# Giving out the PSUM banks anew in the last third of a retention and soft mixture-of-experts kernel

## The chip, the cores and the metric

The kernel runs on one core of one Trainium2 chip. The metric is the device time of one execution in microseconds (us); less is better. The profile is one execution taken by the hardware profiler; its times are counted from the start of its span.

## The reference, cut to what matters

All data are fp32. The attention part is a retention (causal scores with a decay, no softmax) over B = 8, H = 8, S = 576, D = 64. Its output is taken as x with N = 4608 rows and 512 features, and a soft mixture of experts with 8 experts of 4 slots each follows:

```python
logits = x @ phi                              # 4608 x 32
d = exp(logits - logits.max(0)); d /= d.sum(0) + 1e-09
slot_input = (d.T @ x).reshape(8, 4, 512)     # the fold over all rows
for e in range(8):
    h = maximum(slot_input[e] @ w1[e], 0.0)   # 4 x 1024
    slot_out[e] = h @ w2[e]                   # 4 x 512
c = exp(logits - logits.max(1)); c /= c.sum(1) + 1e-09
return c @ slot_out.reshape(32, 512)          # 4608 x 512
```

## The kernel before

The 4608 rows are 36 tiles of 128 rows; four tiles are a group, so there are nine groups (NG = 9). A loop over the 36 tiles (lines 290 to 330) computes the retention of a tile, and, one group late, its logits, its share of the sum over rows (`slot_sums`, with a running maximum) and its combine weights, which stay in `lt`. Everything is scheduled by hand: each engine runs its instructions in the order in which the program issues them, and the framework adds the waits that the data and the PSUM buffers ask for.

Behind the loop come four stages, and the change is in them.

- **The fold** (lines 343 to 397) does the last group. `pm` is a transpose of the maxima, `e_transpose` and `slot_sums` make the group's sums in `acc` (line 262), `dl` and `lrun` (lines 373, 374) rescale them, and two products, `pd` (line 377) and `psi` (line 391), followed by two VectorE operations (line 394), give the experts' inputs `sims`.
- **W1** (lines 420 to 439): 32 weight units of 512 KB stay in SBUF. Eight steps of four units make the two halves of the hidden layer, `ph[:, 0]` and `ph[:, 1]`, two banks of one PSUM tile. A half is copied to `h1` by ScalarE (line 436) and VectorE (line 437). A unit that has been used is released: the buffer takes one of the 19 weight units that are still to come (line 81, on SyncE's queue), or goes to the list `free`.
- **W2** (`expert_2`, line 452): for each half k of the output columns 16 units of 512 KB are summed up in one PSUM tile; `slot_out(k)` copies it (line 458), multiplies it by a selection matrix (line 462) and copies the result to `so` (line 463).
- **Results** (`final(k, g)`, lines 467 to 479): for each k and each of the nine groups four products (eight PE instructions, line 474) fill one half, 256 columns of each bank, of two PSUM tiles of two banks, `po[0]` and `po[1]`. ScalarE copies `po[0]` (line 476), VectorE `po[1]` (line 477) into a free SBUF buffer, and SyncE issues its 512 KB store (line 478). There are 18 of these. Those of k = 0 are strewn between the W2 units of k = 1, one result after every two units; those of k = 1 come at the end, one after another.

PSUM has eight banks. The pool `ps_x` has two buffers of two banks (tiles named sx), `ps_st` one bank (pst), `ps_t` three banks (pt), given out in turn. The pools stay as they are to the end, so the results use the four banks of `ps_x` all the time.

Of the kernel before, what the change touches and what calls it, by code (L numbers as in the profile page):

```python
# [8 lines left out]
F32 = mybir.dt.float32  # L9
# [6 lines left out]
P = 128  # L16
# [3 lines left out]
NS = NE * NSE  # L20
NCH = 5
NT = 36
NG = NT // 4
# [3 lines left out]
W = 256  # L27
# [10 lines left out]
def retention_softmoe(ctx, tc, qkv, wts, phi, mtab, vtab, gtab, ctab, msel, out):  # L38
    nc = tc.nc
    PS = bass.MemoryType.PSUM  # L40
# [3 lines left out]

    cpool = ctx.enter_context(tc.tile_pool(name="cpool", bufs=1))
    small = ctx.enter_context(tc.tile_pool(name="small", bufs=2))
    ps_x = ctx.enter_context(tc.tile_pool(name="ps_x", bufs=2, space=PS))
    ps_st = ctx.enter_context(tc.tile_pool(name="ps_st", bufs=1, space=PS))
    ps_t = ctx.enter_context(tc.tile_pool(name="ps_t", bufs=3, space=PS))

    def const(name, *shape):
        return cpool.tile([P, *shape], F32, name=name)
# [16 lines left out]
    lt = const("lt", NG, P)  # L69
# [42 lines left out]
    for a in range(NP):  # L112
        r = slice(0, D) if a % 2 else slice(D, P)
# [91 lines left out]
    def x_transpose(t, pt=None, eng=None):  # L205
        if pt is None:
            pt = ps_t.tile([P, 512], F32, name="pt")
        for a in range(NP):
            nc.tensor.transpose(pt[:, a * P:(a + 1) * P], xT[t][:, a * P:(a + 1) * P], ident)  # L209
        if eng is nc.vector:  # L210
            nc.vector.tensor_copy(out=xT[t], in_=pt)
        else:
            nc.scalar.copy(out=xT[t], in_=pt)  # L213

    def sm(name, n=1):
        return small.tile([P, n], F32, name=name)
# [36 lines left out]
    def slot_sums(g, pp=None):  # L253
        if pp is None:
            pp = ps_t.tile([P, 512], F32, name="pt")
        for i in range(4):
            nc.tensor.matmul(pp[i * NS:(i + 1) * NS, :], lhsT=ens[:, i * NS:(i + 1) * NS], rhs=xT[4 * g + i],  # L257
                             start=True, stop=True, skip_group_check=True)
        if g == 0:
            nc.vector.tensor_copy(out=acc, in_=pp)  # L260
        else:
            nc.vector.scalar_tensor_tensor(out=acc, in0=acc, scalar=galpha[g], in1=pp, op0=ALU.mult, op1=ALU.add)
# [3 lines left out]
    def comb_1(g):  # L266
        pn = ps_t.tile([P, 512], F32, name="pt")[:, 0:P]
        nc.tensor.transpose(pn, lt[:, g, :], ident)  # L268
        ln = pn.rearrange("p (i s) -> p i s", i=4)
        cmx = sm("cmx", 4)  # L270
        nc.vector.tensor_reduce(out=cmx, in_=ln, axis=AX.X, op=ALU.max)
        cc = cn.rearrange("p (i s) -> p i s", i=4)
        nc.vector.tensor_tensor(out=cc, in0=ln, in1=cmx.unsqueeze(2).broadcast_to([P, 4, NS]), op=ALU.subtract)
        nc.scalar.activation(out=cn, in_=cn, func=AF.Exp, scale=1.0)

    def comb_2(g):
        cc = cn.rearrange("p (i s) -> p i s", i=4)
        sv = sm("csm", 4)
        nc.vector.tensor_reduce(out=sv, in_=cc, axis=AX.X, op=ALU.add)
        nc.vector.tensor_scalar(out=sv, in0=sv, scalar1=1e-9, scalar2=None, op0=ALU.add)  # L280
        ri = sm("cri", 4)
        nc.vector.reciprocal(out=ri, in_=sv)
        nc.vector.tensor_tensor(out=cc, in0=cc, in1=ri.unsqueeze(2).broadcast_to([P, 4, NS]), op=ALU.mult)

    def comb_3(g):
        pc = ps_t.tile([P, 512], F32, name="pt")[:, 0:P]
        nc.tensor.transpose(pc, cn, ident)
        nc.scalar.copy(out=lt[:, g, :], in_=pc)
# [3 lines left out]
    for i in range(NT):  # L292
        g, r = divmod(i - 4, 4)
# [20 lines left out]
        if i == NT - 1:  # L314
            pl = ps_st.tile([P, 512], F32, name="pst")[:, 0:P]
# [21 lines left out]
    sims = rg[2]  # L337
# [3 lines left out]
    sims = sims.rearrange("p (k c e s) -> p k c e s", k=2, c=2, e=NE)  # L341

    g = NG - 1
# [9 lines left out]
    nc.scalar.activation(out=ets, in_=pl, func=AF.Exp, bias=nn, scale=1.0, accum_out=rs)  # L353
    x_transpose(4 * g + 2, eng=nc.vector)
    x_transpose(4 * g + 3, eng=nc.vector)
    pm = ps_t.tile([P, 512], F32, name="pt")[:, 0:P]
    nc.tensor.transpose(pm, nn.broadcast_to([P, P]), ident)
    e_transpose(g)
    alpha = sm("alpha")
# [5 lines left out]
    nc.vector.tensor_tensor(out=nq, in0=nf, in1=far, op=ALU.add)  # L365
    nfp = sm("nfp")
    nc.vector.tensor_reduce(out=nfp, in_=nq, axis=AX.X, op=ALU.min)
    slot_sums(g)
    fa = sm("fa")
    nc.scalar.activation(out=fa, in_=nn, func=AF.Exp, bias=nfp, scale=-1.0)  # L370
    nc.scalar.copy(out=lt[:, g, :], in_=pl)
    dl = sm("dl", NS)
    nc.vector.tensor_scalar(out=dl, in0=delta[:, 0:NS], scalar1=fa, scalar2=None, op0=ALU.mult)
    nc.vector.scalar_tensor_tensor(out=lrun, in0=lrun, scalar=alpha, in1=rs, op0=ALU.mult, op1=ALU.add)
    comb_3(g - 1)
    pd = ps_t.tile([P, 512], F32, name="pt")
    nc.tensor.matmul(pd[:, 0:NS], lhsT=lrun.broadcast_to([P, P]), rhs=dl, start=True, stop=True)
# [4 lines left out]
    def diag(a, n, m):  # L382
        v = a[:, :, 0:1].unsqueeze(3).broadcast_to([P, n, m, NSE])
        ap = [list(x) for x in v.ap]
        ap[2][0] = NS + NSE
        ap[3][0] = 1
        return bass.AP(tensor=v.tensor, offset=v.offset, ap=ap)

    psi = ps_t.tile([P, 512], F32, name="pt")
    for c in range(4):  # L390
        nc.tensor.matmul(psi[:, c * P:c * P + NS], lhsT=acc[:, c * P:(c + 1) * P], rhs=dl, start=True, stop=True,
                         skip_group_check=True)
    for k in range(2):
        nc.vector.tensor_tensor(
            out=diag(sims[:, k].rearrange("p c e s -> p c (e s)"), 2, NE),
# [5 lines left out]
    h1 = rg[1].rearrange("p (n f) -> p n f", n=2)  # L401
    free = []

    def release(t):
        if not load_w(t):
            free.append(t)
# [10 lines left out]
            else:  # L417
                nc.scalar.activation(out=dst, in_=src, func=AF.Relu)

    ph = ps_x.tile([P, 2, 512], F32, name="sx")  # L420
    for n in range(8):
        nh, eh, kp = n // 4, n // 2 % 2, n % 2
        if n == 1:
            comb_1(g)
            comb_2(g)
        if n == 3:
            comb_3(g)
        for c in range(2):
            for i in range(4):
                w = unit_tile[4 * n + i].rearrange("p (c f) -> p c f", c=2)  # L430
                nc.tensor.matmul(ph[i * NS:(i + 1) * NS, nh, :], lhsT=sims[:, kp, c, 4 * eh + i, :], rhs=w[:, c, :],  # L431
                                 start=(n % 4 == 0 and c == 0), stop=(n % 4 == 3 and c == 1), skip_group_check=True)
        for i in range(4):
            release(unit_tile[4 * n + i])
        if n % 4 == 3:
            nc.scalar.copy(out=h1[:, nh, 0:256], in_=ph[:, nh, 0:256])
            nc.vector.tensor_copy(out=h1[:, nh, 256:512], in_=ph[:, nh, 256:512])
        if n == 5:
            hidden_out(0, None)

    so = kts
# [3 lines left out]
    def expert_2(k, n):  # L445
        fh, e = divmod(n, NE)
        if n == 0:
            pp2[k] = ps_t.tile([P, 512], F32, name="pt")[:, 0:W]
        u = unit_tile[32 + k * 16 + n]
        w = u.rearrange("p (c f) -> p c f", c=4)  # L450
        for i in range(4):
            nc.tensor.matmul(pp2[k][i * NS:(i + 1) * NS, :], lhsT=hm[fh][:, i, e, :], rhs=w[:, i, :],  # L452
                             start=(n == 0), stop=(n == 2 * NE - 1), skip_group_check=True)
        release(u)

    def slot_out(k):
        lo, hi = k * W, (k + 1) * W
        nc.scalar.copy(out=p2s[:, lo:hi], in_=pp2[k])
        if k == 0:
            expert_2(1, 0)  # L460
        pso = ps_t.tile([P, 512], F32, name="pt")[:, 0:W]
        nc.tensor.matmul(pso, lhsT=delta, rhs=p2s[:, lo:hi], start=True, stop=True)
        nc.scalar.copy(out=so[:, lo:hi], in_=pso)

    po = [ps_x.tile([P, 2, 512], F32, name="sx") for _ in range(2)]

    def final(k, g):
        lo, hi = k * W, (k + 1) * W
        o = free.pop(0)
        ov = o.rearrange("p (i f) -> p i f", i=4)  # L470
        b = slice(g % 2 * W, (g % 2 + 1) * W)
        for i in range(4):
            r = slice(i * NS, (i + 1) * NS)
            nc.tensor.matmul(po[i // 2][:, i % 2, b], lhsT=lt[r, g, :], rhs=so[r, lo:hi], start=True, stop=True,  # L474
                             tile_position=(i * NS, 0), skip_group_check=True)
        nc.scalar.copy(out=ov[:, 0:2], in_=po[0][:, :, b])  # L476
        nc.vector.tensor_copy(out=ov[:, 2:4], in_=po[1][:, :, b])  # L477
        nc.sync.dma_start(out=out[k, g], in_=o)
        free.append(o)

    for n in range(8):
        expert_2(0, n)
        if n == 1:
            hidden_out(1, None)
    for n in range(8, 16):
        expert_2(0, n)
    slot_out(0)
    n = 1
    for g in range(NG):
        if g:  # L490
            final(0, g - 1)
        for _ in range(2):
            if n < 16:
                expert_2(1, n)
                n += 1
    final(0, NG - 1)
    while n < 16:
        expert_2(1, n)
        n += 1
    slot_out(1)  # L500
    for g in range(NG):
        final(1, g)
    man.close()


# [70 lines left out]
```

## Time and profile before

| | |
|---|---|
| median of 3 runs | 239.07 us (237.6 to 240.0) |
| profiled execution, device time | 237.61 us |
| its span, first to last instruction | 235.8 us |
| busy share of the span: PE, VectorE, ScalarE | 92%, 49%, 33% |
| mean granted TensorE clock | 0.948 of full speed |

PE is TensorE's matmuls and PEld its weight loads, DVE is VectorE, ACT ScalarE, POOL GpSimd, SP SyncE. In the rows a group of instructions is named by line, engine, operation and tiles (written <- read); "x8" is their count, and in brackets stands how long the engine was idle before it and what ended that wait. A granted clock of 1.00 is 2.4 GHz, 0.50 is 1.2 GHz.

### The profile page before, as it was taken

The page shows a single profiled execution, that of the slowest core. Times are in us where ns is not written, and L with a number is a line of the kernel's source. Part 1 is how long each engine was busy: PE and PEld are TensorE (multiplying, and loading weights), DVE is VectorE, ACT ScalarE, POOL GpSimd, SP SyncE. Part 2 cuts the span into 40 slices and gives each one's busy share as a digit, 9 for nine tenths or more (in the row PEclk, how much of TensorE's full clock was granted, in tenths as well). Part 3 has the DMA queues.
Part 4 walks back from the last instruction along what each step waited for, and adds up shares of the span by engine and source line. Part 5 has one row for each costly group of instructions (what it writes and reads, how often), then busy time and mean ns, then how long its engine had stood idle before and what let it go on. Part 6 is the DMA issues. An engine that isn't in the chain of part 4 may idle for free.

```text
span 235.8 us, 8980 instructions
## 1 busy us (share of the span) xinstructions
PE 216.4 (92%) x3994; PEld 160.4 (68%) x3994; DVE 116.3 (49%) x234; ACT 77.5 (33%) x191; POOL 61.2 (26%) x65
## 2 busy tenths in 40 slices
PE   7698879999999999899999999999698999986892
PEld 7587768897897887787897896887432354442450
DVE  1255527667556567738557649557640011343331
ACT  2122334254344353353353452351301012333220
POOL 1544444334244252531353423403100000000000
PEclk9889999999999999999999999999999999996555
DMA  6999978799888889878889887986529999786664
GB/s 199 400 421 406 409 299 273 276 343 360 310 275 315 289 325 344 301 259 289 285 326 353 324 314 277 314 326 220 178 76 410 414 410 375 297 332 272 256 256 202
DMA packets 18181, 72.59 MB, mean 308 GB/s; under 512 B 2272, under 2 KB 2528, under 8 KB 18144
## 3 DMA queue, kind: packets, MB, share of 16 engines
q1 hardware_dynamic: 17568, 71.47, 81.1%
q8 instruction: 31, 0.51, 0.8%
q10 hardware_dynamic: 576, 0.56, 0.7%
q14 instruction: 6, 0.05, 0.1%
HBM read 62.58 MB, written 9.44 MB: 305 GB/s over the span
## 4 chain that ended last, share of the span: by engine, by line
PE 83%; DMA 7%; ACT 3%; DVE 3%; issue 2%; SPq 1%; DVEq 0%
PE sx L189 15%; PE sx L162 11%; PE sx L474 8%; PE pt L153 8%; DMA qb<-in_qkv 7%; PE pt L209 7%; PE sx L431 6%; PE pt L452 6%; PE pst L201 6%; PE sx L181 5%; PE pt L257 3%; PE pt L223 3%; ACT ws L476 2%; PE pst L223 1%; PE pt L268 1%
## 5 line engine op out<-in xcount | busy, mean ns | idle before, releaser
L141 POOL TENSOR_TENSOR qb<-qb,vt 128x512 f32<-128x512 f32 x36 | 37.7, 1048 | 85.8 <-DMA qb<-in_qkv 56.9
L166 DVE TENSOR_TENSOR sts<-sx,mt 128x512 f32<-128x512 f32 x72 | 46.3, 684 | 17.1 <-PE sx L162 17.0
L189 PE MATMUL sx<-sts,qb 128*64 128x128 f32 x576 | 40.5, 283 | 1.0 <-DVE sts L166 0.9
L192 DVE TENSOR_TENSOR rg<-sx,xt 128x512 f32<-128x512 f32 x36 | 24.9, 692 | 29.9 <-PE sx L189 28.3
L154 ACT COPY kts<-pt 128x512 f32<-128x512 f32 x36 | 21.1, 587 | 55.7 <-PE pt L153 53.9
L189 PEld LDWEIGHTS sx<-sts,qb 128*64 128x64 f32 x576 | 31.4, 139 | 11.7 <-issue 6.6
L162 PE MATMUL sx<-qb,kts 64*64 64x64 f32 (+1 forms) x1152 | 32.8, 252 | 0.7 <-ACT kts L154 0.7
L162 PEld LDWEIGHTS sx<-qb,kts 64*64 64x64 f32 x1152 | 27.5, 135 | 3.8 <-ACT kts L154 1.1
L477 DVE COPY ws<-sx 128x512 f32<-128x512 f32 x18 | 12.5, 692 | 28.6 <-PE sx L474 27.7
L153 PE MATMUL pt<-ident,qb 128*128 128x128 f32 x144 | 24.0, 290 | 2.5 <-DMA qb<-in_qkv 2.5
L474 PE MATMUL sx<-kts,lt 32*128 32x256 f32 x144 | 21.9, 561 | 3.2 <-ACT ws L476 2.6
L203 ACT COPY sbs<-pst 128x256 f32<-128x256 f32 x32 | 11.9, 372 | 36.6 <-PE pst L201 36.6
L201 PE MATMUL pst<-qb 128*64 128x64 f32 x512 | 20.7, 225 | 0.0
L181 PE MATMUL sx<-qb,sbs 64*64 64x128 f32 (+1 forms) x512 | 18.2, 257 | 2.7 <-issue 2.7
L153 PEld LDWEIGHTS pt<-ident,qb 128*128 128x128 f32 x144 | 15.5, 143 | 7.5 <-issue 4.8
L474 PEld LDWEIGHTS sx<-kts,lt 32*128 32x128 f32 x144 | 10.9, 237 | 14.0 <-ACT ws L476 11.7
L201 PEld LDWEIGHTS pst<-qb 128*64 128x64 f32 x512 | 19.8, 141 | 0.0
L213 ACT COPY rg<-pt 128x512 f32<-128x512 f32 x33 | 17.9, 597 | 4.4 <-PE pt L209 4.4
L143 POOL TENSOR_TENSOR xt<-gt,cf 128x512 f32<-128x512 f32 x16 | 16.7, 1041 | 8.8 <-DVE rg L192 7.0
L209 PE MATMUL pt<-ident,rg 128*128 128x128 f32 x144 | 18.8, 273 | 0.0
L476 ACT COPY ws<-sx 128x512 f32<-128x512 f32 x18 | 10.5, 586 | 20.9 <-PE sx L474 19.8
L209 PEld LDWEIGHTS pt<-ident,rg 128*128 128x128 f32 x144 | 16.2, 140 | 0.4 <-issue 0.4
(87 smaller groups left out, 177.9 us busy)
## 6 DMA issues: line engine op xcount, KB each, us to landing
ws<-in_wts SPq DMA_DIRECT2D x57, 512.0 KB, 7.0
qb<-in_qkv SPq DMA_DIRECT2D x35, 768.0 KB, 5.8
out<-ws SPq DMA_DIRECT2D x18, 512.0 KB, 2.6
qb<-in_wts SPq DMA_DIRECT2D x6, 512.0 KB, 4.3
qb<-in_qkv SPq DMA_DIRECT2D x3, 256.0 KB, 3.7
sts<-in_wts SPq DMA_DIRECT2D x1, 512.0 KB, 5.0
mt<-in_mtab ACTq DMA_DIRECT2D x1, 256.0 KB, 3.9
gt<-in_gtab ACTq DMA_DIRECT2D x1, 256.0 KB, 7.1
```

What stands on the lines that cost most here:

```text
L141: nc.gpsimd.tensor_tensor(out=v, in0=v, in1=vt[:, c, :].unsqueeze(2).broadcast_to([P, H, D]), op=ALU.mult)
L153: nc.tensor.transpose(pt[:, a * P:(a + 1) * P], part(t, 0)[:, a * P:(a + 1) * P], ident)
L154: nc.scalar.copy(out=kts, in_=pt)
L162: nc.tensor.matmul(sp[R[z], j, a, lo:P], lhsT=kT[R[j], a, z * D:(z + 1) * D], rhs=qT(t)[R[j], a, lo:P], start=True, stop=True, skip_group_ ...
L166: nc.vector.tensor_tensor(out=sT[:, j].rearrange("p (s o) i -> p s o i", s=2), in0=sp[:, j].rearrange("p (s o) i -> p s o i", s=2), in1=m, ...
L181: nc.tensor.matmul(x[R[a % 2], j, a // 2, cols], lhsT=sb[R[j], y, a, :], rhs=qT(t)[R[j], a, cols], start=(a < 2 and y == (0 if z == 2 else ...
L189: nc.tensor.matmul(x[R[a % 2], j, a // 2, :], lhsT=vn(t)[:, 2 * a + j, :], rhs=sT[:, j, a, :], start=(c == 0 and a < 2), stop=True, skip_g ...
L192: nc.vector.tensor_tensor(out=xT[t].rearrange("p (j s i) -> p j s i", j=2, s=2), in0=x, in1=xtab(t).rearrange("p (j s) i -> p j s i", j=2) ...
L201: nc.tensor.matmul(pst[R[j], z, a, :], lhsT=kn(t)[:, 2 * a + j, :], rhs=vn(t)[:, 2 * a + j, :], start=(c == 0 and z == 0 and a == 0), stop ...
L209: nc.tensor.transpose(pt[:, a * P:(a + 1) * P], xT[t][:, a * P:(a + 1) * P], ident)
L213: nc.scalar.copy(out=xT[t], in_=pt)
L474: nc.tensor.matmul(po[i // 2][:, i % 2, b], lhsT=lt[r, g, :], rhs=so[r, lo:hi], start=True, stop=True, tile_position=(i * NS, 0), skip_gro ...
```

## The change

Four edits, all behind the loop over the tiles:

1. In the fold, `pm` takes a buffer of `ps_x` in place of one of `ps_t`. `slot_sums` and the copy of the last logits to `lt` are issued behind `fa`, `dl` and `lrun` and not ahead of them.
2. Ahead of W1 all PSUM pools are closed, and two are opened: `ps_a` with two tiles of two banks, and one of four single banks. The two halves of W1's output are a tile each.
3. `slot_out(0)` has two W2 units ahead of its product and two behind it. The results 0 to 5 of k = 0 are computed in pairs, both halves of the columns of `ps_a`'s tiles at once, with four W2 units behind each pair; 6 and 7 lie inside `slot_out(1)`.
4. Then the four single banks are closed, and a second set, `ps_b`, of two tiles of two banks is opened in their place. Result 8 of k = 0 and the nine of k = 1 use `ps_b` and `ps_a` in turn.

```diff
-    pm = ps_t.tile([P, 512], F32, name="pt")[:, 0:P]
+    pm = ps_x.tile([P, 2, 512], F32, name="sx")[:, 0, 0:P]
...
-    slot_sums(g)
     fa = sm("fa")
     nc.scalar.activation(out=fa, in_=nn, func=AF.Exp, bias=nfp, scale=-1.0)
-    nc.scalar.copy(out=lt[:, g, :], in_=pl)
     dl = sm("dl", NS)
     nc.vector.tensor_scalar(out=dl, in0=delta[:, 0:NS], scalar1=fa, scalar2=None, op0=ALU.mult)
     nc.vector.scalar_tensor_tensor(out=lrun, in0=lrun, scalar=alpha, in1=rs, op0=ALU.mult, op1=ALU.add)
+    slot_sums(g)
+    nc.scalar.copy(out=lt[:, g, :], in_=pl)
     comb_3(g - 1)
...
-    ph = ps_x.tile([P, 2, 512], F32, name="sx")
+    stage.close()
+    ps_a, rest = psum("ps_a", 2), ExitStack()
+    ps_t = rest.enter_context(tc.tile_pool(name="ps_g", bufs=4, space=PS))
+    ph = [ps_a.tile([P, 2, 512], F32, name="po")[:, 0] for _ in range(2)]
...
-                nc.tensor.matmul(ph[i * NS:(i + 1) * NS, nh, :], lhsT=sims[:, kp, c, 4 * eh + i, :], rhs=w[:, c, :],
+                nc.tensor.matmul(ph[nh][i * NS:(i + 1) * NS, :], lhsT=sims[:, kp, c, 4 * eh + i, :], rhs=w[:, c, :],
...
-    def slot_out(k):
+    def slot_out(k, between):
         lo, hi = k * W, (k + 1) * W
         nc.scalar.copy(out=p2s[:, lo:hi], in_=pp2[k])
-        if k == 0:
-            expert_2(1, 0)
+        between[0]()
         pso = ps_t.tile([P, 512], F32, name="pt")[:, 0:W]
         nc.tensor.matmul(pso, lhsT=delta, rhs=p2s[:, lo:hi], start=True, stop=True)
         nc.scalar.copy(out=so[:, lo:hi], in_=pso)
-
-    po = [ps_x.tile([P, 2, 512], F32, name="sx") for _ in range(2)]
...
+        between[1]()
+
+    def final(pool, k, *gs):
         lo, hi = k * W, (k + 1) * W
...
+        po = [pool.tile([P, 2, 512], F32, name="po") for _ in range(2)]
+        os = [free.pop(0) for _ in gs]
+        for n, g in enumerate(gs):
+            for i in range(4):
+                r = slice(i * NS, (i + 1) * NS)
+                nc.tensor.matmul(po[i // 2][:, i % 2, n * W:(n + 1) * W], lhsT=lt[r, g, :], rhs=so[r, lo:hi],
+                                 start=True, stop=True, tile_position=(i * NS, 0), skip_group_check=True)
+        for n, g in enumerate(gs):
+            ov = os[n].rearrange("p (i f) -> p i f", i=4)
+            nc.scalar.copy(out=ov[:, 0:2], in_=po[0][:, :, n * W:(n + 1) * W])
+            nc.vector.tensor_copy(out=ov[:, 2:4], in_=po[1][:, :, n * W:(n + 1) * W])
+            nc.sync.dma_start(out=out[k, g], in_=os[n])
+            free.append(os[n])
...
+    slot_out(0, [lambda: experts_2(1, 0, 2), lambda: experts_2(1, 2, 4)])
+    for g in (0, 2, 4):
+        final(ps_a, 0, g, g + 1)
+        experts_2(1, 2 * g + 4, 2 * g + 8)
+    slot_out(1, [lambda: final(ps_a, 0, 6), lambda: final(ps_a, 0, 7)])
+    rest.close()
+    ps_b = psum("ps_b", 2)
+    final(ps_b, 0, 8)
     for g in range(NG):
...
+        final(ps_b if g % 2 else ps_a, 1, g)
```

## Rows read from the trace of the kernel before

**Rows 1.** The page's forty slices: TensorE clock in tenths, DMA GB/s.

```profile
PEclk9889999999999999999999999999999999996555
GB/s 199 400 421 406 409 299 273 276 343 360 310 275 315 289 325 344 301 259 289 285 326 353 324 314 277 314 326 220 178 76 410 414 410 375 297 332 272 256 256 202
```

**Rows 2.** The timeline in the fold: start, duration, engine, line, operation.

```profile
167.62 0.30 PE L250 MATMUL pt<-ident,ets 128*128 128x128 f32 x1 [0.33 <-DVE rg L211]
...
168.75 0.30 ACT L370 ACTIVATE fa<-nrun,nfp 128x1 f32<-128x1 f32 x1 [0.33 <-DVE nfp L367]
...
169.53 0.75 DVE L262 SCALAR_TENSOR_TENSOR acc<-acc,alpha,pt 128x512 f32<-128x512 f32 x1 [0.82 <-PE pt L257]
...
170.20 0.24 DVE L373 TENSOR_SCALAR dl<-ms,fa 128x32 f32<-128x32 f32 x1
170.34 0.21 DVE L374 SCALAR_TENSOR_TENSOR lrun<-lrun,alpha,rs 128x1 f32<-128x1 f32 x1
...
170.70 0.38 PE L377 MATMUL pt<-dl,lrun 128*128 128x32 f32 x2 [1.10 <-DVE lrun L374]
...
170.92 1.06 PE L391 MATMUL pt<-dl,acc 128*128 128x32 f32 x8
...
172.35 1.92 PE L431 MATMUL sx<-ws,rg 128*32 128x512 f32 x16 [0.37 <-DVE rg L394]
```

**Rows 3.** The timeline in W1: the second half's start, and the reloads.

```profile
174.28 15.39 SPq L81 DMA_DIRECT2D ws<-in_wts  x17
...
181.25 3.64 PE L431 MATMUL sx<-ws,rg 128*32 128x512 f32 x32 [1.03 <-DVE rg L437]
```

**Rows 4.** The chain that ended last, from W2 to the end.

```profile
197.17 0.70 PE pt L462 x2
...
199.51 1.00 PE pt L452 x16
200.51 0.64 PE sx L474 x8
...
209.42 0.59 ACT ws L476
...
210.80 0.59 ACT ws L476
...
217.83 1.25 PE sx L474 x6
```

**Rows 5.** The timeline of the results at full and at half clock.

```profile
198.80 0.71 PE L474 MATMUL sx<-kts,lt 32*128 32x256 f32 x8
...
199.61 0.69 DVE L477 COPY ws<-sx 128x512 f32<-128x512 f32 x1 [8.53 <-PE sx L474]
200.36 32.19 SPq L478 DMA_DIRECT2D out<-ws  x18
...
229.46 0.69 DVE L477 COPY ws<-sx 128x512 f32<-128x512 f32 x1 [1.32 <-PE sx L474]
...
231.47 0.69 DVE L477 COPY ws<-sx 128x512 f32<-128x512 f32 x1 [1.32 <-PE sx L474]
```

**Rows 6.** Windows of 2 us: busy time by engine, clock, DMA share, GB/s.

```profile
212.00:214.00 2.00, 1.12 (x8) 0.31 (x4) 0.69 (x1) 1.02 (x3) 0.00 (x0) 1.00 0.83 336
214.00:216.00 2.00, 1.08 (x10) 0.39 (x10) 0.65 (x1) 0.80 (x2) 0.00 (x0) 0.64 0.66 266
```

**Rows 7.** Windows of 0.25 us, same columns: end of the loads, last store.

```profile
199.50:199.75 0.25, 0.25 (x11) 0.16 (x12) 0.14 (x1) 0.20 (x1) 0.00 (x0) 1.00 1.17 426
199.75:200.00 0.25, 0.25 (x12) 0.16 (x8) 0.25 (x1) 0.25 (x1) 0.00 (x0) 1.00 0.60 230
...
233.00:233.25 0.25, 0.00 (x0) 0.00 (x0) 0.00 (x0) 0.00 (x0) 0.00 (x0) 0.50 0.93 377
...
234.25:234.50 0.25, 0.00 (x0) 0.00 (x0) 0.00 (x0) 0.00 (x0) 0.00 (x0) 0.50 0.27 99
```

**Rows 8.** What the line of the stores shows.

```profile
L478 SPq DMA_DIRECT2D out<-ws x18: 332/332/348, 200.4 to 232.2; - x18
```

More of the change, by code (lines that the diff above doesn't have):

```diff
@@ L46, in retention_softmoe, with psum @@
     small = ctx.enter_context(tc.tile_pool(name="small", bufs=2))
-    ps_x = ctx.enter_context(tc.tile_pool(name="ps_x", bufs=2, space=PS))
-    ps_st = ctx.enter_context(tc.tile_pool(name="ps_st", bufs=1, space=PS))
-    ps_t = ctx.enter_context(tc.tile_pool(name="ps_t", bufs=3, space=PS))
+    stage = ExitStack()
+    def psum(name, bufs):
+        return stage.enter_context(tc.tile_pool(name=name, bufs=bufs, space=PS))
+    ps_x, ps_st, ps_t = psum("ps_x", 2), psum("ps_st", 1), psum("ps_t", 3)
     def const(name, *shape):
@@ L435, in retention_softmoe @@
         if n % 4 == 3:
-            nc.scalar.copy(out=h1[:, nh, 0:256], in_=ph[:, nh, 0:256])
-            nc.vector.tensor_copy(out=h1[:, nh, 256:512], in_=ph[:, nh, 256:512])
+            nc.scalar.copy(out=h1[:, nh, 0:256], in_=ph[nh][:, 0:256])
+            nc.vector.tensor_copy(out=h1[:, nh, 256:512], in_=ph[nh][:, 256:512])
         if n == 5:
@@ L463, in slot_out, with experts_2 @@
         nc.scalar.copy(out=so[:, lo:hi], in_=pso)
-    po = [ps_x.tile([P, 2, 512], F32, name="sx") for _ in range(2)]
-    def final(k, g):
+        between[1]()
+    def final(pool, k, *gs):
         lo, hi = k * W, (k + 1) * W
[L469 to L481, printed above, removed]
+        po = [pool.tile([P, 2, 512], F32, name="po") for _ in range(2)]
[11 more added lines that the diff above has]
+            free.append(os[n])
+    def experts_2(k, lo, hi):
+        for n in range(lo, hi):
+            expert_2(k, n)
+    for n in range(16):
         expert_2(0, n)
@@ L484, in retention_softmoe @@
             hidden_out(1, None)
[L485 to L488, printed above, removed]
-    for g in range(NG):
[L490 to L502, printed above, removed]
+    slot_out(0, [lambda: experts_2(1, 0, 2), lambda: experts_2(1, 2, 4)])
[6 more added lines that the diff above has]
+    final(ps_b, 0, 8)
+    for g in range(NG):
+        final(ps_b if g % 2 else ps_a, 1, g)
+    stage.close()
     man.close()
```

## The prediction

> **What bounds the kernel now.** I read the page first, for clock and traffic by slice [rows 1]; then the chain that ended last, since every edit lies behind the loop over the tiles; then timeline and windows of that stretch.
>
> TensorE sets the pace nearly everywhere, but the last 65 us hold three places where it stands still or another chain sets the pace.
>
> - **The fold.** `psi` stands behind `pd` on PE, and `pd` waits 1.10 us for `lrun`. VectorE has both in order: `acc` from 169.53 to 170.28, then `dl`, then `lrun` at 170.34 [rows 2]. Yet `dl` needs only `fa`, which ScalarE has finished at 169.05. The short operations stand behind the long one that waits for PE.
> - **W1.** The second half's first matmul waits 1.03 us for VectorE's copy of the first half, although that is another bank [rows 3]: the wait comes from the shared tile.
> - **The results.** Among the W2 units PE alternates two units (1.00) with one result (0.64) and never waits [rows 4]. When the units are used up, it waits for each copy: at full clock ScalarE starts one every 1.38 us (209.42, 210.80) [rows 4]; at the end VectorE starts one every 2.01 us (229.46, 231.47), 0.69 of copying and 1.32 of waiting for PE [rows 5]. The same two tiles are written, copied and written again, so PE and copy take turns. In this stretch the granted clock goes from 2.4 to 1.2 GHz: 1.00 up to 214, 0.64 in the next 2 us, then about a half to the end [rows 1, 6].
>
> What lies under that? The W2 loads fill the DMA engines at some 410 GB/s [rows 1] until about 199.9 [rows 7]. All 18 stores come later, from 200.4 to 232.2 [rows 8]. The last, issued at 232.2, moves data from 233.0 to about 234.32 (27% of the last window) [rows 7]: 0.8 us until data flow, 1.30 for 512 KB, and 235.8 - 234.32 = 1.48 to the span's end. Eighteen stores at 1.30 are 23.4 us; they are spread over 33. So a faster chain can gain until the stores stand back to back.
>
> **The change part by part**, against this execution: span 235.8, device time 237.61, so 1.8 around it.
>
> *Fold.* `dl` and `lrun` now come ahead of `acc` on VectorE, so `pd` goes out early, and `psi` waits for `acc` alone. PE took up its work 0.15 us after `lrun`'s end (170.55 to 170.70) [rows 2]; the same lag behind 170.28 gives 170.43 in place of 170.92, a gain of 0.5. `pm` in `ps_x` frees a turn of `ps_t`: the transpose of `ets` had waited 0.33 for VectorE [rows 2], and that goes. Were all of it passed on, the gain would be 0.8; but `acc` now stands behind `dl` (0.24) and `lrun` (0.21), which follow `fa`: 169.05 + 0.45 is 169.50, next to its old start at 169.53. Little is passed on: I take 0.6, bounds 0.5 and 0.8. No instruction changes its place on PE, ScalarE or GpSimd.
>
> *New pools ahead of W1.* New tiles wait for the last reader of their banks. For W1's halves these are readers of `ps_x`, long done; for the single banks, `psi`'s, on which W1 depends anyway. Cost nothing; should closing count as one release of all banks, W1 would wait for the second operation of line 394, a few tenths.
>
> *W1's halves as own tiles.* The 1.03 goes [rows 3]; what is next is the matmul's own turn. I take 1.0; 0 if the wait has another reason. The copies stay hidden behind two more steps. The reloads begin with W1's first releases at 174.28 [rows 3], so they move with the fold alone, and their end comes to 199.9 - 0.6 = 199.3. Their data are there before the units need them: the last unit is used near 207.
>
> *slot_out(0) and pairs.* The first result started at 198.80 [rows 5]. Now it is 1.6 earlier and one unit (0.5) later: 197.7. A pair takes 2 x 0.64 = 1.28 and four units 2.0 [rows 4], so pairs start at 197.70, 200.98 and 204.26. ScalarE (0.59) and VectorE (0.69) copy twice after each pair; from PE's start to VectorE's copy it was 0.81, 0.17 more than the 0.64 [rows 4, 5]. So a pair's copies end 0.17 + 2 x 0.69, about 1.6 us, behind it, and the next pair is 2.0 away: hidden by 0.4. Without that cover it would cost 0.4 a pair, three times.
>
> *slot_out(1).* The last unit ends at 205.54 + 2.0 = 207.54. Result 6 (0.64) covers ScalarE's copy of the W2 sum. Result 7 must wait for 6's copies, for both allocations are `ps_a`: VectorE's run from 208.35 to 209.04. PE stands still some 0.5 us there, but result 7's store is ready at 210.6, and by then stores are queued. `ps_b` waits for the copy to `so`, earlier than result 7.
>
> *The stores*, issued 0.06 behind VectorE's copy (200.30 to 200.36) [rows 5], data 0.8 later:
> results 0 and 1: issued 199.9 and 200.65, data 200.7 to 203.3; 2 and 3: 203.18 and 203.93, 203.98 to 206.6; 4 and 5: 206.46 and 207.21, 207.26 to 209.9; 6: 209.1, 209.9 to 211.2; 7: 210.6, 211.4 to 212.7; 8: 211.4, so behind 7.
> From result 7 on the copies deliver faster than 1.30: at full clock the two sets leave VectorE as the limit, 0.69 and a handover, near 0.8. So ten stores follow back to back: 212.7 + 10 x 1.30 = 225.7, and with the 1.48 the span ends at **227.2**.
>
> *If the clock falls at the end as now*, PE is the limit: 2 x 0.64 = 1.28 a result, an estimate, since no stretch of before shows results unhindered at half clock; six of a result's eight instructions took 1.25 there [rows 4]. From result 7 at 209.1 through result 8 (to 211.7) and nine more, PE ends at 223.2, the last copy near 224.1, data 224.95 to 226.25, span 227.7. The clock hardly matters: the stores cover it.
>
> Sum: 235.8 - 227.2 = 8.6 us less; device time 229.0 against 237.61. That execution is at the lower end of the runs (237.6 to 240.0), so the median moves alike: 239.07 x 229.0 / 237.61 = **230.4**.
>
> By the cause it is made of: most of the 8.6 is the end of PE and copies taking turns; 1.6 from the first two edits would shrink to some 0.6 if the stores stood back to back everywhere, since the loads ahead of them move by the fold only.
>
> **The rule that speaks against it.** Stores that overlap are not in the trace: a lone one flows at 377 GB/s and more in its quarter-microseconds [rows 7], and loads kept about 410 for 25 us [rows 1]. The Trainium skill, "DMA: Bandwidth & Descriptors", section "Where 436 GB/s comes from", says that for transfers between HBM and SBUF the HBM side binds at about 358 GB/s. The loads here don't agree: 410. By that rule a store would take 524,288 bytes / 358 GB/s = 1.46 us, an estimate from that page, and the sum would end about 2 us later.
>
> **The rivals.**
> 1. *Queued stores go slower than a lone one.* For it: nothing shows several in flight. Against: the loads' rate, several in flight, in the same queue. If they sustain 360 GB/s, the 11 stores from result 7 on take 0.16 us more each: 1.7 to 2 us, median 232.3.
> 2. *Two sets in name only*: a result still waits for the copies of the one before, because the framework ties the new pools' tiles together as it tied W1's halves [rows 3]. Then the end keeps its 2.01 us a result at half clock [rows 5]: first VectorE copy of k = 1 near 211.4, the ninth 8 x 2.01 later at 227.5, plus 0.69 + 0.06 + 0.8 + 1.30 + 1.48 gives a span of 231.8 and a median of 235.1. Against: different banks in different pools.
> 3. *Slower: the clock falls at the first pair.* The clock now falls after a stretch in which PE was busy 1.12 of 2 us [rows 6]. If the pairs' bursts made it fall at 197.7, the 9.8 us of PE work to the last unit and the 7.7 of twelve results would take twice as long: 197.7 + 35.0 + some 1.6 of waits = 234.3, and with copy and store (0.2 + 0.69 + 0.06 + 0.8 + 1.30 + 1.48) the span is 238.8, the median 242.1. It decides from a fall ahead of about 200.7; from 207 on it costs nothing. Against: PE is without a gap from 197.7 to 207.5, and units and results alternate at 1.00 in the trace of before. The Trainium skill, "TensorE: Matmul & The Clock Gate", section "A second HAM failure mode: psum-queue depth-cycling", tells of a kernel in which cycling through PSUM banks left PE idle so often that its clock swung between both levels. By that rule this rival would come; the trace agrees only for the stretch behind 210, where PE waits in every result.
>
> **How the numbers follow.** Forecast, stores or PE near 1.3 us a result: 0.73. Rival 1: 0.10. Rival 2: 0.07. Rival 3: 0.05. Else (a wait at the new pools of 2 us or more, a gain of the fold or W1 that fails): 0.05. The forecast's own bounds: fold 0.5 to 0.8, W1 0 to 1.0 (of which the stores pass on at most 1.0), half clock + 0.5, spread of runs - 1.4 to + 1.0: 228.6 to 232.5. With rival 1 the range is 228.0 to 233.2. A measurement of this kernel can tell about 1% from no change, 2.4 us: faster by more holds the forecast, rivals 1 and 2 and most of the rest, 0.89; within 1% 0.05; slower 0.06.
>
> **What would show it.** Right: `psi` 0.5 us or less behind `acc`'s end with `pd` ahead; no wait of line 431 for line 437; pairs without waits; from about 211 to 226 a DMA share near 1.0 and stores that land ever later after their issue, from 0.8 + 1.30 and a little growing to some 8 us at full clock. Wrong: windows of the end at 260 GB/s with gaps (rival 2); full share below 380 GB/s (rival 1); a granted clock of 0.50 ahead of 205 (rival 3); or the first store's issue later than 201, which shifts all stores behind it.

## The result and the profile after

The changed kernel took 231.3 us in the median of 4 runs (231.0 to 237.65), the kernel before 238.33 beside it (237.42 to 240.0); the ratio is 0.969 (95% interval 0.962 to 0.977). The 237.65 is a disturbed execution that the ratio leaves out. Run again in another job, the same program took 228.33 us, ratio 0.954 (0.948 to 0.959). The forecast of 230.4 lies between. The profiled execution took 231.0 us with a span of 229.2.

The page of the changed kernel, as [rows 1]:

```profile
PEclk9889999999999999999999999999997999999975
GB/s 206 387 417 406 409 357 239 251 302 345 322 343 237 274 274 349 321 324 306 280 283 323 329 261 375 298 370 295 206 182 16 378 416 412 407 342 377 396 405 246
```

The last slices, 272 256 256 202 GB/s before, are 377 396 405 246 now. Of the clock's 6555 at the end 75 is left, where PE has nothing more to do. New is a 7 in slice 31: the clock dips at W1's start. The timeline of the fold, as [rows 2]:

```profile
170.00 1.05 DVE L374 TENSOR_SCALAR dl<-ms,fa 128x32 f32<-128x32 f32 x1 [0.36 <-ACT fa L372]
...
170.15 0.90 DVE L375 SCALAR_TENSOR_TENSOR lrun<-lrun,alpha,rs 128x1 f32<-128x1 f32 x1
170.28 0.77 DVE L265 SCALAR_TENSOR_TENSOR acc<-acc,alpha,pt 128x512 f32<-128x512 f32 x1
...
171.20 0.38 PE L380 MATMUL pt<-dl,lrun 128*128 128x32 f32 x2 [0.85 <-DVE acc L265]
...
171.42 1.06 PE L394 MATMUL pt<-dl,acc 128*128 128x32 f32 x8
...
172.85 3.20 PE L437 MATMUL po<-ws,rg 128*32 128x512 f32 x16 [0.37 <-DVE rg L397]
```

`dl` and `lrun` do start ahead of `acc`, but all three end together at 171.05 (start plus duration), and `pd` starts only then. W1's first sixteen matmuls last 3.20 in place of 1.92. The windows of that stretch show the clock at which they ran (columns as [rows 6]):

```profile
168.20:171.20 3.00, 1.80 (x11) 0.59 (x11) 2.42 (x8) 1.17 (x5) 0.95 (x1) 1.00 0.34 130
171.20:172.85 1.65, 1.27 (x11) 1.17 (x11) 0.83 (x4) 0.00 (x0) 0.00 (x0) 1.00 0.00 0
172.85:176.05 3.20, 3.20 (x17) 0.59 (x17) 0.07 (x1) 0.00 (x0) 0.00 (x0) 0.58 0.00 0
```

PE was busy for 1.80 of 3.00 us and then 1.27 of 1.65, at 1.00, and in the first 3.2 us of W1 the granted clock fell from 2.4 to 1.2 GHz (0.58 on average). What made it fall is open, as the experiments show. The timeline of W1, as [rows 3], has the reloads later (176.05, not 174.28) and the second half without a wait, joined to the first in one line:

```profile
176.05 18.27 SPq L84 DMA_DIRECT2D ws<-in_wts  x19
...
180.37 5.36 PE L437 MATMUL po<-ws,rg 128*32 128x512 f32 x48
```

The chain from the first pair on, as [rows 4]:

```profile
200.01 1.07 PE po L478 x16
201.09 1.86 PE pt L458 x32
202.95 1.07 PE po L478 x16
...
210.90 0.59 ACT ws L482
211.49 0.04 issue
211.53 6.25 PE po L478 x63
...
218.54 0.69 DVE ws L483
```

A pair takes 1.07 and four units 1.86, and from 211.53 PE runs eight results almost without a stop, where before each waited for a copy. VectorE and the stores in the timeline, as [rows 5]:

```profile
201.94 21.63 SPq L484 DMA_DIRECT2D out<-ws  x18
...
212.56 1.29 DVE L483 COPY ws<-po 128x512 f32<-128x512 f32 x2 [0.21 <-PE po L478]
```

Two copies take 1.29 with 0.21 of waiting: 0.75 a result, against 2.01 at half clock before. Windows of the end, as [rows 7]:

```profile
212.50:213.00 0.50, 0.50 (x11) 0.29 (x6) 0.44 (x1) 0.50 (x2) 0.00 (x0) 1.00 0.74 295
...
212.50:218.00 5.50, 5.49 (x63) 3.43 (x60) 4.82 (x8) 4.41 (x9) 0.00 (x0) 1.00 0.99 393
218.00:226.00 8.00, 0.49 (x4) 0.09 (x2) 1.02 (x2) 0.41 (x1) 0.00 (x0) 0.70 1.02 407
...
226.50:227.00 0.50, 0.00 (x0) 0.00 (x0) 0.00 (x0) 0.00 (x0) 0.00 (x0) 0.50 0.85 328
227.00:227.50 0.50, 0.00 (x0) 0.00 (x0) 0.00 (x0) 0.00 (x0) 0.00 (x0) 0.50 0.07 25
227.50:228.00 0.50, 0.00 (x0) 0.00 (x0) 0.00 (x0) 0.00 (x0) 0.00 (x0) 0.50 0.04 16
...
227.50:227.75 0.25, 0.00 (x0) 0.00 (x0) 0.00 (x0) 0.00 (x0) 0.00 (x0) 0.50 0.08 33
227.75:228.00 0.25, 0.00 (x0) 0.00 (x0) 0.00 (x0) 0.00 (x0) 0.00 (x0) 0.50 0.00 0
```

All copies are done at 219.2, and the stores run on at full share until 226.9. The last gap in front of them, ahead of result 7's data, ends near 212.65 (a share of 0.74 in that window). The clock is still 1.00 through the results and falls only when PE has nothing left. The line of the stores, as [rows 8] (shortest, middle and longest issue in ns):

```profile
L484 SPq DMA_DIRECT2D out<-ws x18: 332/643/1167, 201.9 to 222.4; - x18
DMA to landing us min/median/max: 2.8/5.0/5.9
```

An issue took 332 to 348 ns before and takes up to 1167 now. The last comes at 222.4, 3.2 us behind its copy: while the stores stand back to back, the issues are held up too.

### The profile page after: what moved, and what is told of

It reads as the page before. It is cut to its first block, busy times and chain, and to the rows that moved or that the text cites. A ratio compares the mean times of both kernels' runs of the same rounds, so it can differ in the third digit from the quotient of the medians.

```text
span 229.2 us, 8978 instructions
## 1 busy us (share of the span) xinstructions
PE 208.5 (91%) x3994; PEld 158.2 (69%) x3994; DVE 115.0 (50%) x234; ACT 77.0 (34%) x191; POOL 61.2 (27%) x65
## 4 chain that ended last, share of the span: by engine, by line
PE 83%; DMA 7%; DVE 3%; issue 2%; SPq 1%; ACT 0%; DVEq 0%
PE sx L192 16%; PE sx L165 11%; PE pt L156 8%; DMA qb<-in_qkv 7%; PE po L437 7%; PE pt L212 7%; PE pt L458 6%; PE pst L204 6%; PE sx L184 5%; PE po L478 5%; PE pt L226 4%; PE pt L260 3%; PE pst L226 1%; PE pt L271 1%; DVE rg L214 1%
## 5 line engine op out<-in xcount | busy, mean ns | idle before, releaser
L165 PE MATMUL sx<-qb,kts 64*64 64x128 f32 (+1 forms) x1152 | 32.6, 250 | 0.7 <-ACT kts L157 0.7
L156 PE MATMUL pt<-ident,qb 128*128 128x128 f32 x144 | 24.5, 294 | 3.2 <-DMA qb<-in_qkv 3.2
L483 DVE COPY ws<-po 128x512 f32<-128x512 f32 x18 | 11.7, 687 | 15.6 <-PE po L478 15.4
L437 PE MATMUL po<-ws,rg 128*32 128x512 f32 x128 | 16.0, 643 | 0.4 <-DVE rg L397 0.4
L184 PEld LDWEIGHTS sx<-qb,sbs 64*64 64x64 f32 x512 | 14.1, 134 | 3.2 <-issue 3.1
L478 PE MATMUL po<-kts,lt 32*128 32x256 f32 x144 | 12.4, 413 | 0.1
```

The source lines that it names most:

```text
L156: nc.tensor.transpose(pt[:, a * P:(a + 1) * P], part(t, 0)[:, a * P:(a + 1) * P], ident)
L165: nc.tensor.matmul(sp[R[z], j, a, lo:P], lhsT=kT[R[j], a, z * D:(z + 1) * D], rhs=qT(t)[R[j], a, lo:P], start=True, stop=True, skip_group_ ...
L184: nc.tensor.matmul(x[R[a % 2], j, a // 2, cols], lhsT=sb[R[j], y, a, :], rhs=qT(t)[R[j], a, cols], start=(a < 2 and y == (0 if z == 2 else ...
L437: nc.tensor.matmul(ph[nh][i * NS:(i + 1) * NS, :], lhsT=sims[:, kp, c, 4 * eh + i, :], rhs=w[:, c, :], start=(n % 4 == 0 and c == 0), stop ...
L478: nc.tensor.matmul(po[i // 2][:, i % 2, n * W:(n + 1) * W], lhsT=lt[r, g, :], rhs=so[r, lo:hi], start=True, stop=True, tile_position=(i * ...
```

## The experiments

Whole times turned out to hold something that no edit touches: the loop over the tiles, the same in all kernels, ended up to 3.4 us apart. In the two profiles of the changed program PE waited there 3.2 us for tile loads where the loop ended later and 1.8 where it ended earlier, and another 2.8 and 2.0 for nothing that the profile shows; why they differ stays open. So I compare stretches of the profiles. Each column is the difference of two starts in the chain: the last logits' products (their x8 piece), W1's first matmul, W2's first, the first result, the end of the span. "Fall" means that the clock fell to 1.2 GHz at W1's start or shortly ahead of it. Each row is one profile; f_half_stores and g_lrun ran only once, and a_fold's profile is of its longest execution (239.45 us). What was expected stands in front of each result, as it was written before the run. The kernel before, run beside each job, had medians from 237.85 to 239.56 us.

| kernel | last logits at | to W1 | W1 | to first result | to the end | sum | time, median us |
|---|---|---|---|---|---|---|---|
| before | 165.17 | 7.18 | 16.69 | 9.83 | 36.97 | 70.67 | 238.33 |
| before_fill | 163.82 | 7.17 | 16.70 | 9.82 | 36.94 | 70.63 | 237.52 |
| a_fold | 167.16 | 6.76 | 18.27 fall | 9.82 | 35.66 | 70.51 | 237.36 |
| b_w1 | 164.78 | 7.18 | 17.04 fall | 9.82 | 37.56 | 71.60 | 238.47 |
| c_results | 164.27 | 7.82 fall | 19.03 fall | 10.12 | 29.27 | 66.24 | 232.15 |
| d_one_set | 165.97 | 6.75 | 17.05 fall | 10.12 | 34.55 | 68.47 | 235.1 |
| changed | 166.09 | 6.76 | 17.04 fall | 10.12 | 29.21 | 63.13 | 231.3 |
| after_again (the same) | 164.16 | 6.76 | 15.46 | 10.13 | 29.38 | 61.73 | 228.33 |
| k_preload | 163.98 | 6.77 | 17.04 fall | 10.12 | 29.19 | 63.12 | 228.67 |
| e_singles | 165.18 | 6.76 | 15.46 | 10.13 | 29.60 | 61.95 | 229.26 |
| f_half_stores | 164.17 | 6.76 | 15.46 | 10.13 | 21.48 | 53.83 | 219.78 |
| h_fill | 164.02 | 6.85 | 15.46 | 10.13 | 28.93 | 61.37 | 227.6 |
| best | 166.23 | 6.85 | 15.46 | 10.13 | 28.97 | 61.41 | 229.83 |
| g_lrun | 163.81 | 6.75 | 15.46 | 10.13 | 29.34 | 61.68 | 227.28 |

The four kernels with one set throughout (the first four rows) differ to the end by the instant at which the clock falls there: 15.7 us behind the first result in before, 19.5 in a_fold, 14.5 in b_w1.

**One part alone.** a_fold is the kernel before with the change's two edits of the fold (the first two pieces of the diff above).

> The kernel before with the edit of the fold alone (pm in ps_x; dl and lrun ahead of acc on VectorE). From the start of the last logits' eight products on the last group's fourth tile to W1's first matmul it took 7.25 us before and 6.83 in the changed kernel. Theory (the fold gives some 0.4 us and the end of this kernel, in which PE and copies take turns, passes it on): 6.8 us, time 0.4 us less than before, which the time alone cannot tell from none. Rival (the 0.6 of the prediction): 6.6 us. Rival (nothing: a later start elsewhere eats it): 7.2 us.

Measured: 6.76 us from the last logits to W1, ratio 0.989 (0.979 to 1.000), which can't be told from none. The theory's 0.4 holds in the stretch. b_w1 gives the halves of W1 a tile each:

```diff
-    ph = ps_x.tile([P, 2, 512], F32, name="sx")
+    ph = [ps_x.tile([P, 2, 512], F32, name="sx")[:, 0] for _ in range(2)]
...
```

> The kernel before with W1's halves as two tiles of ps_x and nothing else. Theory (the wait came from the shared tile): the wait of 1.03 us ahead of the second half is gone, W1 lasts 1.0 us less, time 1.0 us less than before (ratio 0.996). Rival (another reason for the wait): it stands, ratio 1.000.

Ratio 1.001 (0.995 to 1.007), which seems to say that nothing was gained. The chain of b_w1 says otherwise:

```profile
171.96 3.33 PE sx L431 x16
175.29 0.41 PE pt L268
175.70 3.60 PE sx L431 x32
179.30 0.26 PE pt L287
179.56 5.29 PE sx L431 x48
```

The wait is gone, 48 matmuls run in one piece, but the first 16 took 3.33 at the lower clock, 1.41 more than 1.92. With the clock up, in the kernels of the table with this edit and without a fall, W1 lasts 15.46 in place of 16.69, so the edit is worth 1.23. c_results has the new pools, pairs and sets, with fold and `ph` as before.

> The changed kernel with the fold as before and W1's halves in one tile, so the new pools, the pairs and the second set alone. Theory (the end is the first store plus 18 stores back to back; fold and W1 only move the first store): 0.4 + 1.0 us more than the changed kernel, 232.7 us, so five sixths of the gain. Rival (the loads ahead of the stores set the end, which only the fold moves): 0.4 more, 231.7. A lower clock at the start of W1, as the changed kernel's profile has it, would add 1.3 or its absence take 1.3 away.

232.15 us, ratio 0.975 (0.970 to 0.980): between the theory's 232.7 and the rival's 231.7, so the time decides nothing. From the first result to the end it takes 29.27 us, as the changed kernel (29.21). So 7.7 of the gain belong to this part (less the 0.3 by which its first result comes later), and it needs neither of the others. As the end is the same with and without them, the stores also passed on fold and W1 whole.

**Pairs or sets?** d_one_set keeps the pairs and takes `ps_a` throughout:

```diff
+    final(ps_a, 0, 8)
+    for g in range(NG):
+        final(ps_a, 1, g)
     rest.close()
-    ps_b = psum("ps_b", 2)
-    final(ps_b, 0, 8)
-    for g in range(NG):
-        final(ps_b if g % 2 else ps_a, 1, g)
```

> The changed kernel with ps_a for all results, without ps_b: pairs stay, the ten results at the end take turns with their copies. Theory (the second set frees PE from the copies): a result each 1.5 us at full clock, 2.0 if the clock falls as before; the last copy comes 7 to 11 us later than in the changed kernel and the span ends at 231 to 235, time 233 to 237 us. Rival (the pairs ahead of it make the gain, since the stores need 1.3 us each anyway): as the changed kernel, 231.3.

235.1 us, 0.987 (0.980 to 0.994), inside the theory's range; 34.55 from the first result to the end, 5.3 more than with two sets. Its VectorE takes turns with PE, at full and at half clock:

```profile
212.44 0.69 DVE L483 COPY ws<-po 128x512 f32<-128x512 f32 x1 [0.80 <-PE po L478]
213.94 0.69 DVE L483 COPY ws<-po 128x512 f32<-128x512 f32 x1 [0.80 <-PE po L478]
...
222.01 0.69 DVE L483 COPY ws<-po 128x512 f32<-128x512 f32 x1 [1.32 <-PE po L478]
224.03 0.69 DVE L483 COPY ws<-po 128x512 f32<-128x512 f32 x1 [1.33 <-PE po L478]
```

1.50 a result, then 2.02: longer than a store's 1.29. At full clock throughout, the ten results would lose some 2 of the 5.3 us (10 x 0.21, an estimate from these rows); the rest came with the lower clock. e_singles keeps the sets and drops the pairs:

```diff
-    for g in (0, 2, 4):
-        final(ps_a, 0, g, g + 1)
-        experts_2(1, 2 * g + 4, 2 * g + 8)
+    for g in range(6):
+        final(ps_a, 0, g)
+        experts_2(1, 2 * g + 4, 2 * g + 6)
```

> The changed kernel with the results 0 to 5 one by one, each followed by two units, as before, and the second set at the end kept. Theory (the stores behind result 6 stand back to back, so the pairs give nothing): the first store is issued 0.5 us earlier, since the copy needn't wait for the pair's second half; the time is the changed kernel's or up to 0.5 less, 230.8 to 231.3 us. Rival (the pairs are a part of the gain: 2.94 us a pair against 3.28 for two singles): result 6 comes 1.0 later and so does the end, 232.3.

29.60 from the first result to the end, 0.2 to 0.4 more than with pairs: neither as the theory had it (none or less) nor the rival's 1.0. Beside a second set the pairs are worth next to nothing.

**What sets the end?** f_half_stores stores half of each buffer, so half of the output is left out:

```diff
-            nc.sync.dma_start(out=out[k, g], in_=os[n])
+            nc.sync.dma_start(out=out[k, g][:, 0:512], in_=os[n][:, 0:512])
```

> The changed kernel, but every store writes only the first half of its buffer (256 KB), so half of the output is left out. Theory (the stores set the end): the last copy, which ended at 219.2, now sets it: 219.2 + 0.06 + 0.8 + 0.65 + 1.5 to 2.2, a span of 222.2 to 222.9 and a time near 224.4. Rival (PE and the copies set the end): the changed kernel's 231.

From the first result to the end it takes 21.48 us, 7.9 less than after_again with the same PE work. Its last rows, the stores' issues and the last copy:

```profile
198.24 17.04 SPq L484 DMA_DIRECT2D out<-ws  x18
...
215.04 0.69 DVE ws L483
```

The span ends 2.3 us behind the last copy's end (215.73), in the changed kernel 10.0 behind it: the stores set the end. The half that is stored is ScalarE's, so these stores don't wait for VectorE's copy: the last was issued at 214.95 (issues end at 215.28), 0.8 ahead of that copy's end. That is a small part of the 7.9. (The whole span is 218.0, lower than expected by this, the loop and the clock.) k_preload asks whether the loads ahead of the stores matter. It loads two of the 19 late units as halves of 256 KB into `mt`, `gt`, `xts[1]` and `sbs`:

```diff
     load_w(sts)
+    tables = [mt.rearrange("p z o i -> p (z o i)"), gt.rearrange("p a i -> p (a i)"), xts[1].rearrange("p a i -> p (a i)"), sbs]
+    for x, y in (tables[0:2], tables[2:4]):
+        n = len(unit_tile)
+        for h, t in enumerate((x, y)):
+            nc.sync.dma_start(out=t, in_=wts[n][:, h * 512:(h + 1) * 512])
+        unit_tile.append((x, y))
...
```

> The changed kernel with two of the 19 late weight units loaded ahead of W1, into four tables and buffers that are not needed any more, so 17 reloads instead of 19 stand ahead of the stores. The loads end 2.6 us earlier. Theory (the chain to the end is PE up to the first pair, then 18 stores back to back): no change but for a few tenths, 231.0 to 231.4 us. Rival (the stores stand in one row with the loads, so the start of the reloads sets the end): 2.6 us less, 228.7.

The time is the rival's 228.7, and by the time alone I would have taken the rival. The windows of k_preload speak against it:

```profile
195.00:196.50 1.50, 1.50 (x25) 0.81 (x18) 0.00 (x0) 0.37 (x1) 0.00 (x0) 1.00 0.99 393
196.50:198.00 1.50, 1.50 (x22) 0.58 (x25) 0.00 (x0) 0.37 (x1) 0.00 (x0) 1.00 0.23 90
198.00:199.00 1.00, 1.00 (x20) 0.65 (x24) 0.00 (x0) 0.00 (x0) 0.00 (x0) 1.00 0.11 37
199.00:200.50 1.50, 1.50 (x32) 0.86 (x32) 1.29 (x2) 1.07 (x2) 0.00 (x0) 1.00 0.00 0
200.50:202.00 1.50, 1.50 (x28) 0.86 (x24) 0.00 (x0) 0.04 (x1) 0.00 (x0) 1.00 0.89 358
```

The loads do end early, and then the DMA engines move little for some 4 us until the first store; from the first result to the end it is 29.19, as in the changed kernel. Its profiled execution (228.88) is 2.1 us shorter than the changed kernel's (231.0), and its loop ended 2.1 us earlier. after_again settles it.

> The changed kernel once more, beside the two kernels below. Its stretch from the last logits' eight products on the last group's fourth tile to the end took 63.2 us in its first profile and 63.1 in k_preload, whose time was 2.6 us lower because its loop over the tiles ended 2.0 us earlier. Theory (the loop's end varies from run to run by some 2 us, and the late loads don't matter): 63.1 us again where the clock falls at W1's start and 61.8 where it doesn't; time 228.5 to 231.3 us, k_preload's 228.7 within its spread. Rival (k_preload gained by its loads): 231.3 again.

228.33 us: the unchanged program matches k_preload's time. Its clock did not fall, and W1 lasts 15.46; its first sixteen matmuls:

```profile
170.92 1.92 PE po L437 x16
```

**The clock.** h_fill puts four matmuls on `gt` and `ident`, whose results nobody reads, into PE's gaps in the fold:

```diff
     e_transpose(g)
+    pf = ps_x.tile([P, 2, 512], F32, name="sx")
+
+    def fill(*widths):
+        for n in widths:
+            nc.tensor.matmul(pf[:, 0, 0:n], lhsT=ident, rhs=gt.rearrange("p a i -> p (a i)")[:, 0:n], start=True, stop=True)
+
+    fill(128)
...
     comb_3(g - 1)
+    fill(256, 128)
     pd = ps_t.tile([P, 512], F32, name="pt")
```

with another fill(128) behind `psi`.

> The changed kernel with four matmuls more that compute nothing that is used, in a spare buffer of ps_x: one behind the transpose of ets, two ahead of pd, one behind psi, in gaps of PE in the fold. The granted clock of the changed kernel fell to 1.2 GHz for 3.4 us at W1's start, which made W1's first eight of sixteen matmul rows last 3.20 us in place of 1.92. Theory (the gaps of PE in the fold make the clock fall; the first store waits for all of PE's work): the clock stays at 2.4 GHz, W1's first step is 1.3 us shorter, and the end comes 1.3 us earlier: 229.9 us, ratio to the kernel before 0.964 where the changed kernel had 0.969. Rival (the clock falls anyway): 231.3, ratio 0.969. Rival (it doesn't fall, but the stores set the end by the loads ahead of them): reloads start 1.3 earlier too, so the same 229.9; k_preload tells these apart.

227.6 us, ratio 0.954 (0.949 to 0.958), and no fall; but after_again did as well (0.954) without any fill. before_fill has the same in the kernel before.

> The kernel before with h_fill's four matmuls in its fold. Theory (the clock falls at W1's start in some executions of the kernel before as well, and makes a part of its spread from 236.4 to 240): no fall in the profile, time 0 to 1.5 us less than before and never more. Rival (the fill helps the changed kernel alone, by its shorter fold): no difference, or more by the 0.2 that the fill takes where PE wasn't idle.

Ratio 0.993 (0.989 to 0.997), with neither a fall in its profile nor one in before's, and a stretch equal to before's (70.63 and 70.67). The profile shows nothing that would explain the 0.7%; it is within what the loop's end moves. The fall was in six of eleven profiles without the fill and in none of three with it. But four of the six are the four kernels of the first job, which had no fill beside them; in the two jobs that had it, one of five profiles without it fell and none of three with it. That the fill holds the clock is not shown.

**The fold's rest.** g_lrun issues `lrun` ahead of `dl`:

```diff
     nc.vector.tensor_reduce(out=nfp, in_=nq, axis=AX.X, op=ALU.min)
+    nc.vector.scalar_tensor_tensor(out=lrun, in0=lrun, scalar=alpha, in1=rs, op0=ALU.mult, op1=ALU.add)
     fa = sm("fa")
...
-    nc.vector.scalar_tensor_tensor(out=lrun, in0=lrun, scalar=alpha, in1=rs, op0=ALU.mult, op1=ALU.add)
     slot_sums(g)
```

> The changed kernel with lrun issued ahead of dl, nothing else. In the changed kernel dl and lrun began at 170.00 and 170.15, 0.28 and 0.13 ahead of acc, and all three ended with acc at 171.05; pd, which by its semaphore needs dl and lrun alone, began at 171.20. Theory (a short operation that is followed closely by a long one reports its end only with the long one's, so dl is held as well): pd stays 0.15 behind acc's end and the fold gains nothing. Rival (it was lrun, 0.13 ahead of acc, that was not through in time): pd comes 0.8 earlier and psi 0.2, behind acc's end by 0.15.

```profile
167.27 0.21 DVE L371 SCALAR_TENSOR_TENSOR lrun<-lrun,alpha,rs 128x1 f32<-128x1 f32 x1
...
167.72 1.05 DVE L375 TENSOR_SCALAR dl<-ms,fa 128x32 f32<-128x32 f32 x1 [0.24 <-ACT fa L373]
...
167.87 0.90 DVE L265 SCALAR_TENSOR_TENSOR acc<-acc,alpha,pt 128x512 f32<-128x512 f32 x1
...
168.92 0.38 PE L380 MATMUL pt<-dl,lrun 128*128 128x32 f32 x2 [0.85 <-DVE acc L265]
```

`lrun` alone now takes its 0.21, and `dl`, with `acc` 0.15 behind it, takes 1.05 and ends with `acc`; `pd` is held as before. The theory's case: the trace also has the semaphore that `dl` itself raises at 168.79, beside `acc`'s at 168.81. best is h_fill with this edit.

> The kernel h_fill with lrun issued on VectorE ahead of dl, in the time in which dl waits for fa. Theory: 1.3 us less than the changed kernel by the clock, and 0.2 to 0.3 by pd, which is out of psi's way: 1.5 us less than after_again in the same job. Rival (the clock's fall is chance and the fill only moves it): within 0.5 us of after_again.

229.83 us, 1.5 more than after_again in the same job and not less: refuted as a gain. From the last logits on it takes 61.41 against 61.73, but its loop ended 2.1 us later. No complete version here beats the changed kernel by more than that spread.

## Why the prediction was right, point by point

**The end, the main term: right.** From the first pair at 197.70 to the end at 227.2 the prediction had 29.5 us; the two profiles show 29.21 and 29.38. Part of that is luck, for two errors nearly cancel: the pairs were shorter, so result 7's data began 12.6 us behind the first pair (212.65) and not 13.7 (211.4), and the end came 0.8 later behind the last data (below). The bound is the one it named: stores back to back from result 7 on. At 407 GB/s a store of 524,288 bytes takes 1.29, forecast 1.30; f_half_stores and k_preload show that neither PE nor the loads set it. The landing was to grow to some 8 us; from the issue it grew to 5.9, because the issues themselves were held, and from the last copy's end (219.2 to 226.9) it is 7.7. The waiting for copies is what kept the stores apart: with one set it comes back (d_one_set).

**The fold: right mechanism, mis-sized.** The term of 0.6 (bounds 0.5 to 0.8) measured 0.42 (7.18 to 6.76) in every profile with this fold, the fill left aside, whose matmuls take back 0.09. The step that failed is that `pd` would go out early and leave `psi` waiting for `acc` alone. PE's instructions and order are as foreseen, but VectorE reported `dl` and `lrun` only with `acc`, so `psi` came 0.37 behind `acc`'s end and not 0.15. What remains of the gain: `acc` starts 0.17 earlier, as one of the transposes' waits is gone, and the two short operations no longer stand between `acc` and the products.

**W1: right mechanism, a little more.** 1.0 forecast, 1.23 measured at equal clock. The wait of 1.03 was the shared tile's.

**slot_out(0) and the pairs.** One unit later was to cost 0.5; it cost 0.30 (9.83 to 10.13). (The forecast also issued a pair's two stores 0.75 apart, where its own terms give one copy, 0.69; the sum does not hang on it, since their data stand back to back.) A pair with four units takes 2.94 (200.01 to 202.95), not 3.28: on PE longer runs of one kind cost less than the alternation from which the 0.64 and the 1.00 were read. The pairs' copies were hidden as forecast.

**The clock: not the place that was weighed.** The prediction left the clock at the end open, at 0.5 us; it stayed at 2.4 GHz. It had no term for the fold and W1, since in the trace of before the clock was up there. In six of the fourteen profiles it fell, and in the changed kernel's it cost 1.58 us of W1 (17.04 against 15.46): the term that was missing.

**The sum.** 8.6 us forecast; from the last logits to the end 8.94 (70.67 to 61.73) was gained without the fall, 7.54 with it. At the run's end most engines were through at 226.9, but a share of 0.04 to 0.08 ran on to 227.75, and the 1.48 begins only there: the span ended 2.3 behind 226.9. The first profile's span of 229.2 is 2.0 behind the forecast 227.2: 0.9 by the loop (166.09 for 165.17), 1.35 at W1, 0.2 at the fold, less 0.4 at the first result and the end. By the same 0.9 and 1.35 the first store was issued at 201.94, later than the 201 that the prediction had named as a sign of being wrong. That the median still came within 0.9 is luck in part: the forecast scaled 229.0 to 230.4 because the executions before lay above the profiled one, and those of the changed kernel that the ratio counts lay at most 0.4 above theirs.

**The rivals.** Slower queued stores: refuted, 407 GB/s over 8 us. The rule of the Trainium skill in "DMA: Bandwidth & Descriptors", section "Where 436 GB/s comes from", that the HBM side binds at about 358 GB/s, does not hold for these stores on one core either. Two sets in name only: refuted by the 0.75 a result; with one set it was 1.50 (d_one_set). A fall of the clock at the first pair: in no profile of the changed kernel.

## What to carry to other kernels

When one PSUM set takes turns between TensorE and its copies, read two numbers: the period of the turn and the time of the store behind it. A second set pays until the store is the longer one, here 1.50 at full and 2.02 at half clock against 1.29. Once the stores set the end, pairs and earlier loads added nothing here that stands clear of the spread. For edits below 1.5% compare a stretch that begins behind everything common to both kernels; the same program differed by 1.3% between two jobs.

## What the runs showed of the hardware

- **VectorE's short operations ended with the long one close behind them.** In this fold `dl` (128x32) took 0.24 us with only `lrun` behind it [rows 2] and 1.05 when `acc` (128x512) started 0.28 or 0.15 behind it; what waited for it waited for both. The Trainium skill, "VectorE: DVE Perf Modes", section "The DRAIN you can't avoid", says that the next operation does not start until the pipe is empty, but that one which is not held starts earlier. The trace agrees with the second: three operations started within 0.28 us.
- **The clock after a thin stretch is not a property of the program.** The same program showed 0.58 of the clock over W1's first sixteen matmuls in one profile and 1.00 in another, with the same fold of 6.76 us ahead of it. What decides is open.
- **The last store.** About one of the 16 engines (a share of 0.08, 33 GB/s in a quarter-microsecond) ran some 0.8 us longer than the rest, to 227.75, which a mean over 16 engines hides.
- **Issues under a full queue.** A store's issue took 0.33 us with the stores apart [rows 8], and up to 1.17 with them back to back at a share of 1.02.
